# One jump into an arm for all eight experts, instead of one jump per expert

## The chip, the cores and the metric

One core of a Trainium2 chip runs the whole kernel. The metric is device microseconds from launch to end; lower is better.

## What is computed

```python
def reference(q, k, v, f, w_gate, w1, w2, capacity):      # cut to what matters
    # attention: 2 batches, 8 heads, 576 positions, 64 wide; f gives a decay; causal
    scores = q @ k.T / sqrt(64) + decay(f)
    x = softmax(scores) @ v            # -> 1152 tokens of 512
    # mixture of experts: 8 experts, top 1, capacity 288 tokens
    logits = x @ w_gate
    expert_idx = argmax(logits, axis=1);  gate = softmax(logits)[expert_idx]
    # a token takes the next free slot of its expert, and is dropped when there is none
    h = maximum(x_slots[e] @ w1[e], 0)     # w1: 512 x 1024
    y = h @ w2[e]                          # w2: 1024 x 512
    out[token] = gate[token] * y[expert_idx[token], slot[token]]
```

All is float32. How many tokens an expert gets is known only when the routing has been computed on the chip.

## The kernel before

The first 162 us of the span are attention, routing and the beginning of expert 0. That expert's tokens of the first batch, up to 128 of them, are worked through early (`early_*`), and only the rest counts as its load in what follows. The order of this stage comes from a planner in the kernel, and from 162 us on the program's own order holds for TensorE, ScalarE and VectorE.

**An arm.** The work of an expert is written for a fixed number of columns `n`. There are 14 arms: 128, 136, ... 208, 224, 256 and 288 columns. `route` counts the tokens of every expert (`ct`), compares each count with the arms' sizes (`cmp`, `acc`) and so gets the number of the smallest arm that holds them. The old kernel packs the eight numbers into two integers, four bits each (`arm`, two words). Every engine reads both words (`values_load`), and before each expert it cuts the expert's four bits out and jumps to that arm (`tc.Switch`). The code of all 14 arms stands one after the other, and behind the last one the engines meet again, with the next expert's switch. So TensorE, ScalarE, VectorE and GpSimd make two jumps per expert: from the switch to the arm, and from the arm's end to the place where all arms meet. SyncE does not jump: it only issues the weight loads, which stand outside the arms.

**Within an expert** (`expert`), TensorE does:
- L1 (`l1`): eight blocks `f` of 128 hidden rows, each 4 float32 matmuls over the tokens' 512 columns, which the profile counts as 8. Blocks go to three PSUM banks in turn (`a_ps`). ScalarE applies the ReLU and rounds to float32r (`hs[:, f, 0]`), VectorE writes the remainder (`hs[:, f, 1]`), and only then is the bank free.
- The second layer from float32r parts of `w2` and `hs`. At 128 columns it is `l2`, with tokens in the rows: 24 matmuls of 512 columns. At more columns it is `l2t`, with tokens in the columns: 4 blocks of 16 matmuls, then transposes of the result back to token rows (`y_t`).
- The transposes of the next expert's tokens (`x_prep`), which were gathered by index (`gather`, GpSimd).

`w2_split` makes the two parts of `w2`: ScalarE rounds (`w2s[:, 0, k]`), VectorE writes the remainder (`w2s[:, 1, k]`), GpSimd does one of eight. The splits for an expert stand among its own L1 blocks, two ahead of the first ReLU, and there is one buffer `w2s`. The scaled results of an expert go out by index (`y_out`, `scatter`) while the next one's L1 runs.

**Weights.** An expert has four tiles of 1 MB (`load_w`: `u` = 0, 1 are `w1`, 2, 3 are `w2`) in a ring for three experts. The tiles of expert `e + 2` are loaded at the start of expert `e`, into the place of expert `e - 1`.

Of the kernel before, what the change touches and what calls it, by code (L numbers as in the profile page):

```python
# [7 lines left out]
F32 = mybir.dt.float32  # L8
# [3 lines left out]
I32 = mybir.dt.int32  # L12
AF = mybir.ActivationFunctionType
ALU = mybir.AluOpType
AX = mybir.AxisListType
# [6 lines left out]
NE = 8  # L22
FF = 1024
NTOK = B * S
P = 128
# [10 lines left out]
NW1 = 3  # L36
XPD = (3, 3)
EQ = (1, 2)
# [33 lines left out]
ET = mybir.EngineType  # L72
# [9 lines left out]
def arm_sizes(cap):  # L82
    return [a for a in (*range(128, 216, 8), 224, 256) if a < cap] + [cap]
# [3 lines left out]
def attention_moe(ctx: ExitStack, tc: tile.TileContext, cap, kin, rawin, vin, f, c_iw, w1, w2,  # L87
                  c_mask, c_sel, c_idf, c_tri, c_one, c_pri, c_id, c_iota, c_slot, c_arms, out, dbg=None):
    nc = tc.nc
    ctx.enter_context(nc.allow_non_contiguous_dma("small strided loads"))  # L90
    ARMS = arm_sizes(cap)[:-1]
# [6 lines left out]
    wring = {}  # L98

    def open_ring(*keys):  # L100
        for r, u in keys:
            wring[r, u] = ctx.enter_context(tc.tile_pool(name=f"wraw{r}{u}", bufs=2))

    open_ring((0, 0), (0, 1), (1, 0))
    att = ExitStack()
# [299 lines left out]
    def route(b):  # L405
# [25 lines left out]
        for pb in range(b):  # L431
            for i in range(NT):
                r = ROWS[i]
# [72 lines left out]
        if b == 0:  # L506
            nc.vector.tensor_copy(tab[:, :, :, 1:], tg[:, :, :, 1:])
            if NCH > 1:
                nc.vector.tensor_copy(tab[:, :NCH - 1, :, 0], tg[:, 1:, :, 0])
            nc.vector.tensor_reduce(egat, tg[:, 0, :, 0], axis=AX.X, op=ALU.add)  # L510
            nc.vector.scalar_tensor_tensor(oh[:, :, 0], pos, float(P), oh[:, :, 0], op0=ALU.is_ge, op1=ALU.mult)
            emp = rt.tile([P, 1], F32, tag="eemp", name="eemp")
            nc.vector.tensor_scalar(emp, egat, 0.0, BIG, op0=ALU.is_le, op1=ALU.mult)
            nc.vector.tensor_tensor(esix, egix, emp, op=ALU.add)
        else:
            nc.vector.tensor_tensor(tab, tab, tg, op=ALU.add)
            cmp = rt.tile([1, NE, len(ARMS)], F32, tag="cmp", name="cmp")
            nc.vector.tensor_tensor(cmp, ct[:, :, None].to_broadcast([1, NE, len(ARMS)]),
                                    arms[:, None, :len(ARMS)].to_broadcast([1, NE, len(ARMS)]), op=ALU.is_gt)
            acc = rt.tile([1, NE], F32, tag="acc", name="acc")  # L520
            nc.vector.tensor_reduce(acc, cmp, axis=AX.X, op=ALU.add)
            nc.vector.tensor_tensor(acc, acc, arms[:, len(ARMS):], op=ALU.mult)
            pk = rt.tile([1, 2], F32, tag="pk", name="pk")
            nc.vector.tensor_reduce(pk, acc.rearrange("p (a e) -> p a e", a=2), axis=AX.X, op=ALU.add)
            nc.vector.tensor_copy(arm, pk)
        yield

    arms = const.tile([1, len(ARMS) + NE], F32, name="arms")
    arm = const.tile([1, 2], I32, name="arm")
    tab = const.tile([P, NCH, 3, NE], F32, name="tab")  # L530
    tab_i = const.tile([P, NCH, NE], F32, name="tab_i")
    prev = {}
# [56 lines left out]
        nc.vector.scalar_tensor_tensor(h[:, :, 1], a, 0.0, h[:, :, 0].bitcast(F32), op0=ALU.max, op1=ALU.subtract)  # L589

    def load_w(e, u, eng=nc.sync):
        t = wring[e % 3, u // 2].tile([P, 2048], F32, tag="w", name=f"wr{e}_{u}")
        if u < 2:
            eng.dma_start(t, w1[e, :, 2 * u:2 * u + 2, :].rearrange("p k f -> p (k f)"))
        else:
            eng.dma_start(t, w2[e, :, 4 * (u - 2):4 * (u - 2) + 4, :].rearrange("p k d -> p (k d)"))
        raws[e, u] = t
# [194 lines left out]
            t[z] += more  # L792
    act, dve = nc.scalar, nc.vector
    xc = range(min(2, NCH))
    ENG = [ET.PE, ET.Activation, ET.DVE, ET.Pool]

    def width(c):
        return min(P, SC - c * P)
# [25 lines left out]
    with tc.manual_schedule(engines=MAN):  # L824
        for e in (0, 1):
            for c in xc:
                gather(e, c, part(c))
        for k in range(FC):
            if k == EK:
                early_h(1)  # L830
            w2_split(0, k, nc.gpsimd if k in PK else dve)
        for k in range(FC):
            early_l2(k)
            for c in xc:
                if k == XE[c]:
                    x_prep(0, c, [act, dve], [spsum(f"x0{c}"), x_ps0 if c else spsum("x00b")])
            if k == XE[2]:
                packed = [nc.values_load(arm[0:1, z:z + 1], engines=tuple(ENG), min_val=0, max_val=16 ** 4 - 1)
                          for z in range(2)]
        act.activation(yss[0][0], ob_ps, AF.Copy, scale=egat)  # L840
    a_ps, y_ps, q_ps = banks[:3], banks[3:3 + NCH], banks[6:]

# [113 lines left out]
    with tc.manual_schedule(engines={ET.PE, ET.Activation, ET.DVE}):  # L956
        scatter(yss[0][0], esix[:, 0:1])
        for c in xc:
            dve.memset(y_ps[c], 0.0)
        for e in range(NE):  # L960
            for q in ((1, 2) if e == 0 else (e + 2,)):
                for u in range(NW1 if q == 1 else 0, 4 if q < NE else 0):
                    load_w(q, u, nc.sync if e else nc.gpsimd if u in EQ else nc.scalar)
            reg = ((packed[e // 4] >> 4 * (e % 4)) & 15).with_bounds(min_val=0, max_val=len(ARMS))
            for z in tc.Switch({g: reg for g in ENG}, len(ARMS) + 1):
                expert(e, (ARMS + [SC])[z])


def host_arrays(inputs):
# [25 lines left out]
    for i in range(NT):  # L995
# [16 lines left out]
        "c_one": np.ones((P, P), bf),  # L1012
        "c_pri": pri,
        "c_id": ids.astype(bf),
        "c_arms": np.array([arm_sizes(cap)[:-1] + [16 ** (e % 4) for e in range(NE)]], np.float32),
        "c_slot": np.arange(nch * P, dtype=np.float32).reshape(nch, P).T,
        "c_iota": np.broadcast_to(np.arange(cap).astype(np.float16), (P, cap)),
    }
# [20 lines left out]
```

## Time and profile before

| | |
|---|---|
| time, median of 3 runs | 381.79 us (381.0 to 383.2) |
| span of the profiled execution | 374.9 us (the page gives no other time of it) |
| TensorE busy | 311.3 us, 83% |
| VectorE / ScalarE / GpSimd busy | 182.3 / 153.5 / 118.5 us |
| L847, the matmuls of L1 | 81.4 us busy, 49.3 us idle before them |

The span runs from the first to the last instruction on the core. Busy time is summed over the whole span; what an engine waits for, and where, is in the views of the trace. In them `PE` is TensorE's matmuls, `PEld` its weight loads, DVE is VectorE, ACT ScalarE, POOL GpSimd and SP SyncE; a name with a small q behind it (`DVEq`) is the engine's sequencer. "Issue" is time in which an engine waited for nothing that the profile shows.

### The profile page before, as it was taken

What the parts mean: (1) busy time and instruction counts of PE and PEld (TensorE: products, weight loads), DVE (VectorE), ACT (ScalarE), POOL (GpSimd) and SP (SyncE); (2) the same over time, 40 slices, a digit from 0 to 9 for tenths busy, and PEclk for the clock granted to TensorE, in tenths of its full rate; (3) what the DMA queues carried; (4) which work ended last, traced back from release to release, by engine and by line L of the source; (5) the groups of instructions that cost most, each with busy time, mean ns of one, the idle gap of its engine ahead of it and who ended that gap; (6) DMA issues with size and microseconds to landing.
All of it is one profiled execution on the core that took longest, in us unless ns stands there. A gap on an engine that the chain in (4) does not pass through costs nothing.

```text
span 374.9 us, 6090 instructions
## 1 busy us (share of the span) xinstructions
PE 311.3 (83%) x1952; PEld 242.0 (65%) x1953; DVE 182.3 (49%) x605; ACT 153.5 (41%) x416; POOL 118.5 (32%) x142
## 2 busy tenths in 40 slices
PE   7999999999999999998659558758658397877980
PEld 3555666566565656988459558757557396877980
DVE  6565667579884654673116107208053251722520
ACT  4364666666663655352044116106241433513510
POOL 4458456673547100254022203203231220300301
PEclk8599999999996999999989969969969879996997
DMA  8993996799271941438992760583917600000001
GB/s 166 252 225 101 251 370 177 138 294 366 62 200 32 388 185 31 146 93 298 410 353 99 270 237 35 203 299 116 405 43 288 243 4 11 30 8 7 34 5 47
DMA packets 19747, 64.86 MB, mean 173 GB/s; under 512 B 3503, under 2 KB 7231, under 8 KB 15074
## 3 DMA queue, kind: packets, MB, share of 16 engines
q1 hardware_dynamic: 12354, 44.86, 36.5%
q0 software_dynamic: 6224, 15.21, 14.8%
q10 hardware_dynamic: 1040, 3.44, 2.5%
q8 instruction: 36, 0.59, 0.7%
q14 instruction: 93, 0.76, 0.6%
HBM read 56.38 MB, written 9.10 MB: 175 GB/s over the span
## 4 chain that ended last, share of the span: by engine, by line
PE 60%; issue 17%; DMA 14%; DVE 4%; ACT 1%; ACTq 1%; DVEq 1%; POOL 0%; SPq 0%; POOLq 0%
DMA out<-yss,six 12%; PE bank L847 11%; PE bank L312 9%; PE bank L269 8%; PE bank L339 7%; PE bank L268 6%; PE bank L882 4%; PE bank L355 3%; PE bank L862 3%; PE bank L577 2%; PE bank L781 1%; DMA wr<-in_w 1%; DMA raw<-in_rawin 1%; PE bank L399 1%; PE bank L819 1%
## 5 line engine op out<-in xcount | busy, mean ns | idle before, releaser
L847 PE MATMUL bank<-xs,wr 128*128 128x128 f32 (+3 forms) x512 | 81.4, 326 | 49.3 <-issue 20.5
L847 PEld LDWEIGHTS bank<-xs,wr 128*128 128x128 f32 x512 | 78.4, 222 | 53.3 <-issue 32.2
L777 DVE TENSOR_TENSOR w2s<-wr,w2s 128x512 fp32r<-128x512 f32 x56 | 44.7, 816 | 74.7 <-ACT w2s L776 54.5
L776 ACT ACTIVATE w2s<-wr 128x512 fp32r<-128x512 f32 x64 | 38.9, 628 | 71.7 <-PE bank L847 40.6
L294 ACT ACTIVATE p<-p,nb 128x128 f32<-128x128 f32 (+4 forms) x80 | 47.6, 597 | 9.6 <-DVE nb L282 9.5
L907 POOL DMA_INDIRECT out<-yss,six x16 | 16.0, 1002 | 108.8 <-ACT yss L899 101.3
L325 ACT ACTIVATE p<-bank 128x256 f32<-128x256 f32 (+4 forms) x56 | 24.8, 448 | 37.3 <-PE bank L312 36.8
L282 DVE CUSTOM_DVE_ANT_0 p<-bank,cd 128x128 f32<-128x128 f32 (+2 forms) x64 | 31.1, 486 | 18.4 <-PE bank L269 10.5
L312 PE MATMUL bank<-idf,p 128*128 128x128 f32 (+2 forms) x240 | 39.2, 276 | 0.4 <-ACT p L294 0.4
L268 PE MATMUL bank<-hi 128*128 128x128 f32 (+5 forms) x96 | 38.1, 397 | 1.6 <-POOL hi L245 1.6
L269 PE MATMUL bank<-kl,hi 64*128 64x128 f32 (+5 forms) x96 | 38.0, 396 | 0.0
L862 PE MATMUL bank<-hs,w2s 128*128 128x304 f32 (+2 forms) x128 | 34.5, 352 | 0.0
L852 ACT ACTIVATE hs<-bank 128x128 fp32r<-128x128 f32 (+3 forms) x64 | 18.5, 293 | 34.6 <-PE bank L847 30.6
L807 POOL DMA_INDIRECT xg<-x_dram,gix x16 | 15.6, 977 | 53.6 <-PE bank L819 19.2
L312 PEld LDWEIGHTS bank<-idf,p 128*128 128x128 f32 (+2 forms) x240 | 23.2, 139 | 14.3 <-issue 5.9
L864 PE MATMUL bank<-hs,w2s 128*128 128x152 f32 (+2 forms) x128 | 30.6, 239 | 0.0
L339 PE MATMUL bank<-p,v 128*64 128x320 f32 (+4 forms) x224 | 30.4, 390 | 0.0
L241 POOL TENSOR_TENSOR kl<-raw,hi 64x576 fp32r<-64x576 f32 x15 | 21.5, 1437 | 15.0 <-PE bank L269 6.4
L269 PEld LDWEIGHTS bank<-kl,hi 64*128 64x128 f32 (+1 forms) x96 | 16.2, 169 | 15.5 <-issue 11.6
L853 DVE SCALAR_TENSOR_TENSOR hs<-bank,hs 128x128 fp32r<-128x128 f32 (+3 forms) x64 | 19.0, 304 | 15.0 <-ACT hs L852 14.8
L882 PE MATMUL bank<-w2s,hs 128*128 128x512 f32 x96 | 25.2, 405 | 0.0
L268 PEld LDWEIGHTS bank<-hi 128*128 128x128 f32 (+1 forms) x96 | 17.4, 181 | 11.4 <-issue 3.9
(142 smaller groups left out, 414.4 us busy)
## 6 DMA issues: line engine op xcount, KB each, us to landing
wr<-in_w SPq DMA_DIRECT2D x27, 1024.0 KB, 12.7
raw<-in_rawin SPq DMA_DIRECT2D x7, 576.0 KB, 8.1
hi<-in_kin POOLq DMA_DIRECT2D x7, 576.0 KB, 12.4
cd<-c_dram SPq DMA_DIRECT2D x7, 576.0 KB, 9.5
wr<-in_w ACTq DMA_DIRECT2D x3, 1024.0 KB, 10.9
v<-in_vin SPq DMA_DIRECT2D x8, 320.0 KB, 4.3
out<-zero SPq DMA_DIRECT2D x8, 288.0 KB, 5.4
wr<-in_w POOLq DMA_DIRECT2D x2, 1024.0 KB
```

Of the source, the lines that this page charges most:

```text
L268: nc.tensor.matmul(s[:r, :cw], qa, hi[:, j, KA + c0:KA + c0 + cw], start=True, stop=False)
L269: nc.tensor.matmul(s[:r, :cw], qa[:D], kl[:, j, c0:c0 + cw], start=False, stop=True)
L282: nc.vector.tensor_tensor_reduce(p[:r, a:b], s[:r, a - c0:b - c0], src[:r, a:b], -0.125, 1e30 if a == 0 else nb[:r, 0:1], ALU.add, ALU.min ...
L294: nc.scalar.activation(p[:r, :w], p[:r, :w], AF.Exp, bias=bias, scale=-1.0, accum_out=rsum[:r, h // 2 % 2, i, h % 2:h % 2 + 1])
L312: nc.tensor.transpose(t[:kw, c * r:(c + 1) * r], p[:r, c * P:c * P + kw], idf[:r, :r])
L339: nc.tensor.matmul(o[a * D:a * D + D, c0:w], vt[g][:kw, a, c], ps[a][:kw, c, c0:w], start=(c == 0), stop=(c == nk - 1), skip_group_check=True)
L776: nc.scalar.activation(w2s[:, 0, k], raw, AF.Copy)
L777: eng.tensor_tensor(w2s[:, 1, k], raw, w2s[:, 0, k].bitcast(F32), op=ALU.subtract)
L847: nc.tensor.matmul(a[:, :n], w[:, (k % 2) * FF + f * P:(k % 2) * FF + (f + 1) * P], xs[e % 2][k // 2][:, k % 2, :n], start=(k == 0), stop= ...
L862: nc.tensor.matmul(av, w2s[:, 0, k, ds], hs[:, k, :, :n], start=(k == 0), stop=(k == FC - 1), skip_group_check=True)
L864: nc.tensor.matmul(av[:, 0], w2s[:, 1, k, ds], hs[:, k, 0, :n], start=False, stop=(k == FC - 1), skip_group_check=True)
L882: nc.tensor.matmul(y_ps[0][:n], hs[:, k, y, :n], w2s[:, z, k], start=(k == 0 and z + y == 0), stop=(k == FC - 1 and z == 1))
```

## The change

One number is kept instead of eight: the largest over the experts. There is one switch, ahead of expert 0, and each of the 14 arms holds all eight experts one behind the other, all with the same `n`. The weight loads now stand inside the arms, so SyncE jumps too (`ENG`). The weight tiles are twelve fixed buffers where the old kernel drew each from a pool; in both, two tiles share a ring place as before.

```diff
     def open_ring(*keys):
         for r, u in keys:
-            wring[r, u] = ctx.enter_context(tc.tile_pool(name=f"wraw{r}{u}", bufs=2))
+            pool = ctx.enter_context(tc.tile_pool(name=f"wraw{r}{u}", bufs=1))
+            wring[r, u] = [pool.tile([P, 2048], F32, name=f"wr{r}{2 * u + z}") for z in range(2)]
...
             acc = rt.tile([1, NE], F32, tag="acc", name="acc")
             nc.vector.tensor_reduce(acc, cmp, axis=AX.X, op=ALU.add)
-            nc.vector.tensor_tensor(acc, acc, arms[:, len(ARMS):], op=ALU.mult)
-            pk = rt.tile([1, 2], F32, tag="pk", name="pk")
-            nc.vector.tensor_reduce(pk, acc.rearrange("p (a e) -> p a e", a=2), axis=AX.X, op=ALU.add)
+            pk = rt.tile([1, 1], F32, tag="pk", name="pk")
+            nc.vector.tensor_reduce(pk, acc, axis=AX.X, op=ALU.max)
             nc.vector.tensor_copy(arm, pk)
...
     def load_w(e, u, eng=nc.sync):
-        t = wring[e % 3, u // 2].tile([P, 2048], F32, tag="w", name=f"wr{e}_{u}")
+        t = wring[e % 3, u // 2][u % 2]
...
-    ENG = [ET.PE, ET.Activation, ET.DVE, ET.Pool]
+    ENG = [ET.PE, ET.Activation, ET.DVE, ET.Pool, ET.SP]
...
-                packed = [nc.values_load(arm[0:1, z:z + 1], engines=tuple(ENG), min_val=0, max_val=16 ** 4 - 1)
-                          for z in range(2)]
+                chosen = nc.values_load(arm[0:1, 0:1], engines=tuple(ENG), min_val=0, max_val=len(ARMS))
...
-        for e in range(NE):
-            for q in ((1, 2) if e == 0 else (e + 2,)):
-                for u in range(NW1 if q == 1 else 0, 4 if q < NE else 0):
-                    load_w(q, u, nc.sync if e else nc.gpsimd if u in EQ else nc.scalar)
-            reg = ((packed[e // 4] >> 4 * (e % 4)) & 15).with_bounds(min_val=0, max_val=len(ARMS))
-            for z in tc.Switch({g: reg for g in ENG}, len(ARMS) + 1):
+        for q in (1, 2):
+            for u in range(NW1 if q == 1 else 0, 4):
+                load_w(q, u, nc.gpsimd if u in EQ else nc.scalar)
+        for z in tc.Switch({g: chosen for g in ENG}, len(ARMS) + 1):
+            for e in range(NE):
+                if e and e + 2 < NE:
+                    for u in range(4):
+                        load_w(e + 2, u)
                 expert(e, (ARMS + [SC])[z])
```

VectorE between expert 0 and expert 1, before: these rows are the last of expert 0's arms (the copies of the next x), the jump, the registers of the next switch, and the start of expert 1's first arm (L777 is the second half of `w2_split`, L853 the second half of `hs`).

```order
L804 COPY xs_1875<-bank_81 128x2x128
L804 COPY xs_1875<-bank_82 128x2x80
L1035 UNCONDITIONAL_BRANCH
L1035 SWITCH_STRIDE
L1035 REGISTER_ALU x2
L1035 ISA x2
L965 BRANCH_PREFETCH_HINT
L777 TENSOR_TENSOR w2s<-wr_2_1863,w2s 128x512 x2
L853 SCALAR_TENSOR_TENSOR hs<-bank_75,hs 128x128
```

The same place in the changed kernel, in the arm of 200 columns (there, lines behind L838 are one less):

```order
L867 TENSOR_REDUCE yt<-bank_86 128x200
L804 COPY xs_1879<-bank_81 128x2x128
L804 COPY xs_1879<-bank_83 128x2x80
L777 TENSOR_TENSOR w2s<-wr_1856,w2s 128x512 x2
L852 SCALAR_TENSOR_TENSOR hs<-bank_81,hs 128x200
```

The jump out, the switch's rows and the jump in are gone, and the first split of the next expert stands right behind the copies.

ScalarE at the one switch, before: the read of the arms' words, the scaling of expert 0's early rows, the three weight loads that ScalarE issues, the switch and the first arm.

```order
L838 TENSOR_LOAD arm x2
L840 ACTIVATE yss_1878<-bank_81,egat 128x512
L596 DMA wr_3_1979<-in_w 128x2048
L594 DMA wr_0_1981<-in_w 128x2048
L596 DMA wr_3_1987<-in_w 128x2048
L1035 SWITCH_STRIDE
L1035 REGISTER_ALU
L1035 ISA x2
L965 BRANCH_PREFETCH_HINT
L852 ACTIVATE hs<-bank_75 128x128
```

And in the changed kernel up to the switch, then the start of the tenth arm:

```order
L838 TENSOR_LOAD arm
L839 ACTIVATE yss_1882<-bank_87,egat 128x512
L596 DMA wr_1857<-in_w 128x2048
L594 DMA wr_1861<-in_w 128x2048
L596 DMA wr_1867<-in_w 128x2048
L1036 SWITCH_STRIDE
L1036 ISA x2
```

```order
L962 BRANCH_PREFETCH_HINT
L851 ACTIVATE hs<-bank_81 128x200
L851 ACTIVATE hs<-bank_82 128x200
```

The rows ahead of the switch are the same but for one read and one register row less; nine arms of eight experts each stand between them and the tenth arm.

SyncE's queue behind the attention stage, before: the last load that stands ahead of the experts, then the four loads of expert 3.

```order
L596 DMA wr_2_1863<-in_w 128x2048
L1035 UNCONDITIONAL_BRANCH
L594 DMA wr_0_3974<-in_w 128x2048
L594 DMA wr_1_3976<-in_w 128x2048
L596 DMA wr_2_3978<-in_w 128x2048
L596 DMA wr_3_3980<-in_w 128x2048
```

And now:

```order
L596 DMA wr_1856<-in_w 128x2048
L838 TENSOR_LOAD arm
L838 ISA x2
L1036 SWITCH_STRIDE
L1036 ISA x2
L962 BRANCH_PREFETCH_HINT
L594 DMA wr_66<-in_w 128x2048
L594 DMA wr_67<-in_w 128x2048
L596 DMA wr_71<-in_w 128x2048
L596 DMA wr_72<-in_w 128x2048
```

The four loads are the same; SyncE reads the arm's number and jumps before them.

## Rows read from the trace of the kernel before

**Rows 1.** The page: the span, and the chain of work that ended last, by engine.

```profile
span 374.9 us, 6090 instructions
...
PE 60%; issue 17%; DMA 14%; DVE 4%; ACT 1%; ACTq 1%; DVEq 1%; POOL 0%; SPq 0%; POOLq 0%
```

**Rows 2.** TensorE's matmuls in order of time over the expert stage: start us, us, line, operation, output<-input, weights, columns, how many; in brackets the idle time before and what ended it. L847 is L1, L882 the second layer at 128 columns, L862 (with L864) the second layer of the wider arms, L891 the transposes of its result.

```profile
168.65 2.84 PE L847 MATMUL bank<-xs,wr 128*128 128x128 f32 x24
172.81 4.73 PE L847 MATMUL bank<-xs,wr 128*128 128x128 f32 x40 [1.33 <-DVE hs L853]
177.30 2.33 PE L882 MATMUL bank<-w2s,hs 128*128 128x512 f32 x9
...
181.54 2.33 PE L882 MATMUL bank<-w2s,hs 128*128 128x512 f32 x9
188.47 4.96 PE L847 MATMUL bank<-xs,wr 128*128 128x152 f32 x24 [4.60 <-issue]
196.61 5.43 PE L847 MATMUL bank<-xs,wr 128*128 128x152 f32 x40 [3.18 <-DVE hs L853]
201.78 0.40 PE L862 MATMUL bank<-hs,w2s 128*128 128x304 f32 x1
...
209.94 0.38 PE L891 MATMUL bank<-idf,yt 128*128 128x128 f32 x2
...
218.88 5.11 PE L847 MATMUL bank<-xs,wr 128*128 128x152 f32 x24 [7.18 <-DMA wr<-in_w]
...
247.05 5.46 PE L847 MATMUL bank<-xs,wr 128*128 128x128 f32 x24 [5.60 <-issue]
...
268.55 2.92 PE L847 MATMUL bank<-xs,wr 128*128 128x128 f32 x24 [2.78 <-issue]
276.02 6.87 PE L847 MATMUL bank<-xs,wr 128*128 128x128 f32 x40 [4.56 <-DVE hs L853]
...
292.01 2.92 PE L847 MATMUL bank<-xs,wr 128*128 128x128 f32 x24 [2.81 <-issue]
...
315.14 3.50 PE L847 MATMUL bank<-xs,wr 128*128 128x160 f32 x24 [2.23 <-ACT w2s L776]
319.82 5.70 PE L847 MATMUL bank<-xs,wr 128*128 128x160 f32 x40 [1.18 <-DVE hs L853]
325.25 0.41 PE L862 MATMUL bank<-hs,w2s 128*128 128x320 f32 x1
...
333.53 0.38 PE L891 MATMUL bank<-idf,yt 128*128 128x128 f32 x2
...
334.47 0.82 PE L891 MATMUL bank<-idf,yt 128*128 128x128 f32 x6
339.97 13.72 PE L847 MATMUL bank<-xs,wr 128*128 128x200 f32 x64 [4.69 <-issue]
353.39 0.48 PE L862 MATMUL bank<-hs,w2s 128*128 128x400 f32 x1
...
362.91 1.20 PE L891 MATMUL bank<-idf,yt 128*128 128x128 f32 x8
```

**Rows 3.** The chain that ended last, in order of time: start us, us, what it spent it on. The first row is at the boundary from expert 0 to expert 1, the next three from expert 3 to expert 4, the last from expert 5 to expert 6.

```profile
188.08 6.69 issue
...
264.23 5.05 issue
269.29 0.04 DVEq L1035
...
269.64 4.63 issue
...
311.37 2.91 issue
```

**Rows 4.** Stretches of the trace: from and to in us, length, busy time of TensorE's matmuls and weight loads, DVE, ACT and POOL with counts, then the granted TensorE clock, the mean share of the 16 DMA engines, GB/s.

```profile
189.00:194.00 5.00, 4.43 (x24) 4.20 (x22) 0.00 (x0) 3.48 (x9) 0.35 (x1) 0.72 1.02 348
276.00:279.00 3.00, 2.98 (x14) 2.98 (x15) 2.45 (x6) 0.81 (x3) 0.00 (x0) 0.50 0.01 1
312.90:316.00 3.10, 0.86 (x7) 0.89 (x7) 0.00 (x0) 1.15 (x2) 0.00 (x0) 1.00 0.05 11
```

**Rows 5.** ScalarE in order of time in expert 7 (200 columns): the evictions of L1's blocks; two of the same kind stand between these two. Columns as in rows 2.

```profile
349.74 0.34 ACT L852 ACTIVATE hs<-bank 128x200 fp32r<-128x200 f32 x1
...
353.80 0.34 ACT L852 ACTIVATE hs<-bank 128x200 fp32r<-128x200 f32 x1 [1.02 <-PE bank L847]
```

**Rows 6.** All engines in order of time at the start of expert 7: ScalarE's first two splits and VectorE's first `hs`.

```profile
341.02 1.15 ACT L776 ACTIVATE w2s<-wr 128x512 fp32r<-128x512 f32 x2 [6.19 <-PE bank L847]
...
343.43 0.37 DVE L853 SCALAR_TENSOR_TENSOR hs<-bank,hs 128x200 fp32r<-128x200 f32 x1
```

**Rows 7.** All engines in order of time around the switch of expert 0: VectorE's last work ahead of it, ScalarE's last weight load ahead of it, ScalarE's first work behind it.

```profile
169.30 1.02 DVE L959 MEMSET bank<- 128x512 f32 x2 [0.87 <-DVE xs L804]
...
170.70 0.45 ACTq L596 DMA_DIRECT2D wr<-in_w  x1
...
172.09 0.61 ACT L852 ACTIVATE hs<-bank 128x128 fp32r<-128x128 f32 x3 [2.52 <-PE bank L847]
```

**Rows 8.** The page, DMA issues: what is loaded, by which queue, how many, KB each, median us from issue to landing.

```profile
wr<-in_w SPq DMA_DIRECT2D x27, 1024.0 KB, 12.7
```

**Rows 9.** Waits from 165 us to the end: who waited for whom, us in total, times, longest.

```profile
PE bank L847 <- DVE hs L853: 19.4, 7, 4.6
```

More of the change, by code (lines that the diff above doesn't have):

```diff
@@ L518, in route @@
             nc.vector.tensor_tensor(cmp, ct[:, :, None].to_broadcast([1, NE, len(ARMS)]),
-                                    arms[:, None, :len(ARMS)].to_broadcast([1, NE, len(ARMS)]), op=ALU.is_gt)
+                                    arms[:, None, :].to_broadcast([1, NE, len(ARMS)]), op=ALU.is_gt)
             acc = rt.tile([1, NE], F32, tag="acc", name="acc")
             nc.vector.tensor_reduce(acc, cmp, axis=AX.X, op=ALU.add)
-            nc.vector.tensor_tensor(acc, acc, arms[:, len(ARMS):], op=ALU.mult)
-            pk = rt.tile([1, 2], F32, tag="pk", name="pk")
-            nc.vector.tensor_reduce(pk, acc.rearrange("p (a e) -> p a e", a=2), axis=AX.X, op=ALU.add)
+            pk = rt.tile([1, 1], F32, tag="pk", name="pk")
+            nc.vector.tensor_reduce(pk, acc, axis=AX.X, op=ALU.max)
             nc.vector.tensor_copy(arm, pk)
         yield
-    arms = const.tile([1, len(ARMS) + NE], F32, name="arms")
-    arm = const.tile([1, 2], I32, name="arm")
+    arms = const.tile([1, len(ARMS)], F32, name="arms")
+    arm = const.tile([1, 1], I32, name="arm")
     tab = const.tile([P, NCH, 3, NE], F32, name="tab")
@@ L1014, in host_arrays @@
         "c_id": ids.astype(bf),
-        "c_arms": np.array([arm_sizes(cap)[:-1] + [16 ** (e % 4) for e in range(NE)]], np.float32),
+        "c_arms": np.array([arm_sizes(cap)[:-1]], np.float32),
         "c_slot": np.arange(nch * P, dtype=np.float32).reshape(nch, P).T,
```

## The prediction, made before the changed kernel was run

> **What bounds the kernel now.** I read the page first. In the chain that ended last, TensorE has 60% of the span and "issue" 17% [rows 1]: a sixth of the span is time in which an engine on the chain waited for nothing that the profile shows. To place it I read TensorE's order of time over the expert stage, which begins at 168.65 us with the first L1 matmul of expert 0 [rows 2]. Here the reader is to see two things.
>
> First, the widths. The experts' L1 matmuls are 128, 152, 152, 128, 128, 128, 160 and 200 columns wide: the old kernel fits every expert to its own tokens, and the largest arm is 200.
>
> Second, the holes. From expert 1 on each expert's L1 comes after 2.2 to 7.2 us of idle engine, and in most a second hole of 1.2 to 4.6 us stands between the first 24 matmuls and the other 40, put down to DVE's `hs` [rows 2]. Before the first kind nothing is late by the profile; in the second, DVE is late, because it had a hole of its own. The chain shows DVE's between experts 3 and 4: 5.05 us of issue, then 0.35 us in which its sequencer works on the next switch (269.29 to 269.64), then 4.63 us of issue [rows 3]. So each boundary has two jumps, out of the arm and into the next one. Their price goes with the DMA load: 6.69 us at the boundary where the DMA engines are full (share 1.02), 2.91 us where they are nearly empty (share 0.05) [rows 3, 4]. TensorE's holes are shorter than DVE's since it still has queued matmuls to run. So every engine is bound here by its jumps and not by its work, and that is what the change touches.
>
> **What the jumps cost now.** I take the work of an expert without holes and subtract. All stretches are at the full granted clock, from start to start [rows 2].
> - L1 is 64 matmuls; 40 of them take 177.30 - 172.81 = 4.49 us at 128 columns, 5.17 us at 152 and 5.43 us at 160. Times 1.6: 7.18, 8.27, 8.69 us. At 200 columns ScalarE's evictions, one per 8 matmuls, stand 353.80 - 349.74 = 4.06 us apart for three [rows 5]: 1.353 us x 8 = 10.83 us.
> - The second layer: 181.54 + 2.33 - 177.30 = 6.57 us at 128 columns (other form, preparation of the next x included); 8.16 us at 152; 8.28 us at 160; 362.91 - 353.39 = 9.52 us at 200.
> - The transposes after it, in the wide form alone: 334.47 + 0.82 - 333.53 = 1.76 us.
>
> An expert is then 13.75 us at 128, 18.19 at 152, 18.73 at 160 and 22.11 at 200. Experts 0 to 6 are 4 x 13.75 + 2 x 18.19 + 18.73 = 110.1 us of work, but they take 339.97 - 168.65 = 171.3 us. [...]
>
> **The change, part by part.**
>
> *Seven boundaries go: -61.2 us.* Inside the arm no engine jumps between experts. What must then be in time is ScalarE's and DVE's chain to the first `hs`, since TensorE has three banks and stops at the fourth block, 3 x 1.353 = 4.06 us after its L1 begins. Expert 7 shows this chain at the same width: from ScalarE's first split at 341.02 to DVE's `hs` at 343.43 + 0.37 = 343.80 it takes 2.78 us [rows 6]. Without jumps ScalarE is free as soon as it has copied the next x, before L1 begins, so the chain has 1.3 us to spare. I take no hole. The bound from the other side is the shortest hole left in the old trace, 1.18 us [rows 2]: 7 x 1.18 = +8.3 us.
>
> *Padding: +44.7 us.* Experts 0 to 6 run at 200 columns: 7 x 22.11 = 154.8 us for 110.1. ScalarE, DVE and POOL grow too, but expert 7 shows TensorE's L1 as the pace at that width: ScalarE's evictions wait for it.
>
> *Expert 7: -2.6 us.* It now enters without a hole. Its L1 took 353.39 - 339.97 = 13.42 us, all of it without a hole [rows 2]; at full clock it is 10.83 us, as above.
>
> *One entry: +8.3 us.* In the old kernel expert 0's arm is the first, right behind the switch, and ScalarE goes through in 172.09 - 171.15 = 0.94 us [rows 7]. Now all engines jump to the tenth arm. ScalarE can do so only after its three weight loads are issued, 170.70 + 0.45 = 171.15 [rows 7]. By then the loads are on the way, so I price the jump as the dear one: 171.15 + 0.4 + 6.69 = 178.2; plus one eviction of 0.34 (ScalarE) and 0.37 us (DVE) [rows 5, 6] TensorE's fourth block starts at 178.9. Without a hole it would start at 168.65 + 24 x 0.169 = 172.7: 6.2 us late. DVE, free at 170.32, is not later. Behind a hole of that size I charge a half clock as behind expert 4's, 6.87 - 4.73 = 2.1 us. TensorE's own jump, earlier and shorter, lies inside this. Bounds: with the cheapest jump (2.91 us) the block starts 2.4 us late and no clock is lost, +2.4 us; with DVE's two-jump hole of some 12 us the loss is 11.5 + 2.1 = 13.6 us.
>
> *Nothing for the loads and the registers.* SP now jumps too and issues the loads inside the arm. Expert 3's go when expert 0's L1 is over, near 187, and are used a period and a half later, near 243; a load lands in 12.7 us [rows 8]. If that cover went, expert 3 would wait up to those 12.7 us, once. One value is read where two were unpacked; the 0.35 us of switch rows per boundary lie in the 61.2.
>
> Sum: -61.2 + 44.7 - 2.6 + 8.3 = **-10.8 us**; the span goes from 374.9 to 364.1. The page gives no time of this execution but its span; the runs' median is 381.79 (381.0 to 383.2), 6.9 us above, and I leave that as it is, as the tail behind expert 7's last transposes: 381.79 - 10.8 = **371.0 us**.
>
> [...]
>
> **Rivals.**
> - *The holes are no jumps and stay.* Only the padding would be paid: 381.79 + 44.7 = 426 us. [...] Against it: the holes stand on each side of the register rows of the switch, and expert 0, whose arm needs no jump, has none on ScalarE. 0.01.
> - *The second hole stays (slower).* `w2s` has one buffer, so the splits begin only when the last second-layer matmuls are done. If the first `hs` still comes late as before, TensorE loses 19.4 us in seven holes [rows 9], and the sum is 371.0 + 19.4 = 390 us, more with a half clock. It decides from 10.8 / 7 = 1.5 us per boundary, which needs the chain to end 5.6 us after L1's start. For it: the trace names `hs` as what ended these holes. Against it: expert 7 has no such hole at the same width. 0.05. A shorter one of up to 1.2 us, to 379 us: 0.13.
> - *TensorE's code doesn't arrive in a straight line (slower).* One stall per expert at the cheapest jump's 2.91 us is 8 x 2.91 = 23 us: 394 us; it decides from 1.4 us. Against it: inside the arms of the wide experts there is no hole from the 25th matmul to the last transposes. 0.03.
> - *The entry hides:* 371.0 - 5.9 = 365 us. For it: the loads are only issued from 169 on. 0.12.
>
> That the arm is not 200 is no case: 200 is the widest of the eight shapes in the trace.
>
> **The numbers.** The forecast (367 to 374 us) has 0.66. The range runs from the hidden entry to the short holes, 365.5 to 379 us, and leaves out the slower rivals and the ends. A change of 0.5% (1.9 us) is about what can be told from none here: faster 0.87, same 0.05 (the upper end of the short holes), slower 0.08.
>
> **What would show it.** Eight experts with L1 at 200 columns, some 22.1 us from start to start from expert 1 on; no issue hole in TensorE but one at the entry; ScalarE's first eviction near 178 instead of 172.09; the clock at 1.00 from expert 1 on; loads of expert 3 from about 187. I am wrong if periods are 24 us or more, if DVE's `hs` still ends waits at the boundaries, or if issue holes stand inside the arm.

## The result and the profile after

The changed kernel takes 357.6 us (median of 5 runs, 357.3 to 363.9) beside 381.79 us for the old one (375.9 to 385.1): a ratio of 0.9455, with a 95% interval of 0.934 to 0.957. I forecast faster, but at 371.0 us, in a range of 365.5 to 379.0. The gain is 24.2 us by the medians and 357.6 / 0.9455 - 357.6 = 20.6 us by the ratio, where I had 10.8, so the size is wrong and the time lies below the range.

In some executions, of either kernel, the clock granted over the whole run is lower and the time longer (0.949 and 363.94 us beside 0.960 to 0.970 and 357.3 to 358.9 us in the changed kernel, 0.855 and 396.78 us beside 0.920 and 376.18 us in the old one); the ratios leave those out and the medians do not, the first profile of the changed kernel (a span of 362.1 us) is such a one, and so I take lengths of the stage before the experts from its other profiles.

The page of the changed kernel: the span, two DMA queues that carry instructions (packets, MB, share of 16 engines), and the two groups that answer to what the old kernel waited for.

```profile
span 362.1 us, 6223 instructions
...
PE 344.1 (95%) x2144; PEld 279.8 (77%) x2145; DVE 191.9 (53%) x612; ACT 164.2 (45%) x436; POOL 118.6 (33%) x142
...
q8 instruction: 19, 0.31, 0.3%
q14 instruction: 25, 0.20, 0.2%
...
L846 PE MATMUL bank<-xs,wr 128*128 128x200 f32 x512 | 90.0, 337 | 4.5 <-issue 2.9
...
L777 DVE TENSOR_TENSOR w2s<-wr,w2s 128x512 fp32r<-128x512 f32 x56 | 46.4, 845 | 9.6 <-ACT w2s L776 9.5
```

The same rows before:

```profile
q8 instruction: 36, 0.59, 0.7%
q14 instruction: 93, 0.76, 0.6%
...
L777 DVE TENSOR_TENSOR w2s<-wr,w2s 128x512 fp32r<-128x512 f32 x56 | 44.7, 816 | 74.7 <-ACT w2s L776 54.5
```

Of what the instruction queues moved less than half is left, 0.51 MB for 1.35. L1's matmuls had 49.3 us of idle time before them and have 4.5. VectorE waited 54.5 us for ScalarE's half of the splits and waits 9.5.

TensorE's order of time answers to [rows 2]; L846 is L1, L861 the first row of the second layer, L890 the transposes. First from the entry to expert 2, then expert 7.

```profile
171.21 0.95 PE L781 MATMUL bank<-w2s,he 128*128 128x512 f32 x3
175.03 5.98 PE L846 MATMUL bank<-xs,wr 128*128 128x200 f32 x24 [2.87 <-issue]
182.66 7.03 PE L846 MATMUL bank<-xs,wr 128*128 128x200 f32 x40 [1.65 <-DVE hs L852]
...
200.49 10.99 PE L846 MATMUL bank<-xs,wr 128*128 128x200 f32 x64
211.18 0.49 PE L861 MATMUL bank<-hs,w2s 128*128 128x400 f32 x1
...
220.70 0.38 PE L890 MATMUL bank<-idf,yt 128*128 128x128 f32 x2
...
222.29 10.99 PE L846 MATMUL bank<-xs,wr 128*128 128x200 f32 x64
...
331.22 10.99 PE L846 MATMUL bank<-xs,wr 128*128 128x200 f32 x64
...
351.42 1.20 PE L890 MATMUL bank<-idf,yt 128*128 128x128 f32 x8
```

The reader is to see that both kinds of holes are gone from expert 1 on: L1 is one run of 64 matmuls, and from start to start it is (331.22 - 200.49) / 6 = 21.79 us. Both remain once, at the entry. The windows say the same (from and to, length, busy TensorE matmuls and weight loads, DVE, ACT, POOL, granted clock, DMA share, GB/s):

```profile
222.30:331.20 108.90, 108.90 (x722) 108.90 (x721) 53.33 (x105) 47.59 (x116) 23.66 (x23) 1.00 0.38 145
```

Over five experts TensorE is busy all of the time, at the full clock, with the DMA engines at 0.38. One caution: the chain that ended last still shows 19% of issue, but its longest pieces lie inside such a stretch, as at 296.81:

```profile
296.81 16.55 issue
```

By the window above TensorE works all through it, so nothing stands still there.

### The profile page after: what moved, and what is told of

Same layout as the page of the kernel before. It is cut to its first block, busy times and chain, and to the rows that moved or that the text cites. A ratio compares the mean times of both kernels' runs of the same rounds, so it can differ in the third digit from the quotient of the medians.

```text
span 362.1 us, 6223 instructions
## 1 busy us (share of the span) xinstructions
PE 344.1 (95%) x2144; PEld 279.8 (77%) x2145; DVE 191.9 (53%) x612; ACT 164.2 (45%) x436; POOL 118.6 (33%) x142
## 4 chain that ended last, share of the span: by engine, by line
PE 70%; issue 19%; POOL 3%; DVE 3%; DMA 2%; ACTq 1%; ACT 0%; SPq 0%; POOLq 0%; DVEq 0%
PE bank L846 14%; PE bank L313 9%; PE bank L861 9%; PE bank L270 8%; PE bank L340 8%; PE bank L269 7%; PE bank L863 4%; PE bank L356 3%; PE bank L400 2%; DMA raw<-in_rawin 2%; POOL out L906 1%; DVE w2s L777 1%; PE bank L577 1%; PE bank L819 1%; POOL w2s L777 1%
## 5 line engine op out<-in xcount | busy, mean ns | idle before, releaser
L846 PE MATMUL bank<-xs,wr 128*128 128x200 f32 x512 | 90.0, 337 | 4.5 <-issue 2.9
L846 PEld LDWEIGHTS bank<-xs,wr 128*128 128x128 f32 x512 | 88.0, 193 | 5.2 <-issue 3.3
L861 PE MATMUL bank<-hs,w2s 128*128 128x400 f32 x256 | 76.6, 367 | 0.0
L863 PE MATMUL bank<-hs,w2s 128*128 128x200 f32 x256 | 65.2, 255 | 0.0
L777 DVE TENSOR_TENSOR w2s<-wr,w2s 128x512 fp32r<-128x512 f32 x56 | 46.4, 845 | 9.6 <-ACT w2s L776 9.5
L863 PEld LDWEIGHTS bank<-hs,w2s 128*128 128x128 f32 x256 | 49.0, 191 | 0.0
L861 PEld LDWEIGHTS bank<-hs,w2s 128*128 128x128 f32 x256 | 48.1, 188 | 0.0
L851 ACT ACTIVATE hs<-bank 128x200 fp32r<-128x200 f32 x64 | 21.4, 337 | 41.8 <-PE bank L846 26.8
L852 DVE SCALAR_TENSOR_TENSOR hs<-bank,hs 128x200 fp32r<-128x200 f32 x64 | 23.0, 362 | 29.8 <-ACT hs L851 29.6
L870 DVE TENSOR_TENSOR yt<-bank,yt 128x200 f32<-128x200 f32 x24 | 8.8, 366 | 46.9 <-ACT yt L869 46.9
L869 ACT ACTIVATE yt<-bank 128x200 f32<-128x200 f32 x24 | 8.1, 337 | 47.6 <-PE bank L863 47.6
```

The costliest lines, as they stand in the source:

```text
L777: eng.tensor_tensor(w2s[:, 1, k], raw, w2s[:, 0, k].bitcast(F32), op=ALU.subtract)
L846: nc.tensor.matmul(a[:, :n], w[:, (k % 2) * FF + f * P:(k % 2) * FF + (f + 1) * P], xs[e % 2][k // 2][:, k % 2, :n], start=(k == 0), stop= ...
L861: nc.tensor.matmul(av, w2s[:, 0, k, ds], hs[:, k, :, :n], start=(k == 0), stop=(k == FC - 1), skip_group_check=True)
L863: nc.tensor.matmul(av[:, 0], w2s[:, 1, k, ds], hs[:, k, 0, :n], start=False, stop=(k == FC - 1), skip_group_check=True)
```

## The experiments

All times are medians of runs beside the old kernel on the same chip. L781 is the last work of the stage before; from its end to the end of the span is the expert stage, the quantity that the change touches. It is 374.9 - 168.8 = 206.1 us in the old kernel and 362.1 - 172.16 = 189.9 us in the changed one.

**The changed kernel again, without an edit (`again`).**

> The changed kernel as it is, once more, for a second profile. In the first one the span is 362.1 us, while other runs of it are 6 us shorter. Theory A (the attention stage of that one execution was slow, clock 0.74 from 20 to 40 us, and the expert stage is what it is): the expert stage, from the last early matmul to the end, is again 190 us (189.9), periods of 21.8 us from expert 1 on, and a shorter span comes from an earlier start of it, near 166 to 169 us. Theory B (the expert stage itself varies): the stage is some 184 us and begins near 172 us.

Measured: 358.21 us (356.7 to 358.8), a ratio of 0.9487 (0.9388 to 0.9586). The expert stage is 354.9 - 166.13 = 188.8 us, 1.1 us from the first profile's, although the span is 7.2 us shorter. So the expert stage repeats, and what differs lies ahead of it.

**All experts on the largest arm, with the jumps left in (`pad`).** The old kernel; `route` packs the largest of the eight numbers eight times.

```diff
-            nc.vector.tensor_tensor(acc, acc, arms[:, len(ARMS):], op=ALU.mult)
+            top = rt.tile([1, 1], F32, tag="top", name="top")
+            nc.vector.tensor_reduce(top, acc, axis=AX.X, op=ALU.max)
+            nc.vector.tensor_tensor(acc, top.to_broadcast([1, NE]), arms[:, len(ARMS):], op=ALU.mult)
```

> The kernel before, with its eight switches, but every expert takes the arm of the largest count (200 columns): the padding alone. Theory J (the holes are the jumps' own, and as long as before): the padding costs 7 x 21.8 - 110.1 = 42.5 us and expert 0 pays one jump more: 420 to 430 us. Rival H (in the narrow arms TensorE only waited for VectorE and ScalarE, so that part of the wider work fits into the holes): 395 to 410 us, with shorter holes than 8.7 us per boundary.

Measured: 432.86 us (429.1 to 439.5), a ratio of 1.1439 (1.103 to 1.1848). TensorE's order of time, L1 of experts 0, 1, 2, 6 and 7 (here L849):

```profile
169.96 5.74 PE L849 MATMUL bank<-xs,wr 128*128 128x200 f32 x24 [3.12 <-issue]
...
202.02 6.76 PE L849 MATMUL bank<-xs,wr 128*128 128x200 f32 x24 [7.81 <-issue]
...
235.43 7.12 PE L849 MATMUL bank<-xs,wr 128*128 128x200 f32 x24 [7.62 <-DMA wr<-in_w]
...
365.48 13.72 PE L849 MATMUL bank<-xs,wr 128*128 128x200 f32 x64 [5.15 <-issue]
...
395.37 12.44 PE L849 MATMUL bank<-xs,wr 128*128 128x200 f32 x64 [5.21 <-issue]
```

With the same 200 columns as in the changed kernel a period is (395.37 - 169.96) / 7 = 32.2 us (29.8 to 33.5) instead of 21.79. The padding is paid, and 10.4 us of boundary on top of it, so the holes belong to the jumps and not to the widths. They are longer than the old kernel's (171.3 - 110.1) / 7 = 8.7 us, and the time lies above theory J's 420 to 430 us, which had them as long as before. The fixed weight buffers, which came with the change, have no run of their own; `noload`, below, draws no weight tile from expert 3 on, and VectorE's two jumps still take 5.5 and 7.0 us there at two boundaries, so the buffers are at most a part of it.

**The straight line without the padding (`fit`).** The changed kernel; the tenth arm gives each expert its own width, written out for the token counts of these inputs.

```diff
+FIT = [128, 152, 152, 128, 128, 128, 160, 200]
...
-                expert(e, (ARMS + [SC])[z])
+                expert(e, FIT[e] if z == 9 else (ARMS + [SC])[z])
```

> The changed kernel, but the tenth arm holds the eight experts at their own widths (128, 152, 152, 128, 128, 128, 160, 200, fixed for this input): the jumps alone, no padding. Theory J, with the work without holes as worked out from the trace (13.75, 18.19, 18.73 us): 42.5 us less than the changed kernel, near 315 us. Rival H (at 128 columns VectorE's split and eviction, some 1.1 us per block, are slower than TensorE's 0.9, and the first eviction comes late): L1 of the 128-column experts near 9 to 11 us instead of 7.2, 320 to 330 us. Rival D (4 MB of weights per 14 us don't arrive in time): TensorE waits for loads, over 325 us.

Measured: 319.66 us (314.0 to 337.2), a ratio of 0.8461 (0.8208 to 0.8715). L1 of experts 1, 2, 3, 6 and 7:

```profile
186.33 8.43 PE L847 MATMUL bank<-xs,wr 128*128 128x152 f32 x64
204.26 8.43 PE L847 MATMUL bank<-xs,wr 128*128 128x152 f32 x64
222.19 7.67 PE L847 MATMUL bank<-xs,wr 128*128 128x128 f32 x64
...
262.94 8.85 PE L847 MATMUL bank<-xs,wr 128*128 128x160 f32 x64
281.40 10.99 PE L847 MATMUL bank<-xs,wr 128*128 128x200 f32 x64
```

There are no holes at these widths either, nor at experts 4 and 5 between, and the time is near theory J's 315 us. L781's counterpart ends at 164.47, so the expert stage is 312.2 - 164.47 = 147.7 us. That is 188.8 - 147.7 = 41.1 us below `again`: the padding by itself, where I had 44.7. From expert 1's L1 to the end it is (354.9 - 193.35) - (312.2 - 186.33) = 35.7 us, where the sum had 36.3; the rest of the miss lies at expert 0, where TensorE's second hole is 2.37 us in `fit` and 0.44 in `again`, so part of the wider work falls into the entry's wait. Against the old kernel the stage is 206.1 - 147.7 = 58.4 us shorter: the jumps by themselves with the entry paid, where the sum had 61.2 + 2.6 - 8.3 = 55.5. `pad` keeps the jumps and `fit` leaves the padding out; the two parts of the sum are each seen alone.

**The arm right behind the switch (`first`, and `first_b` with more runs).** The changed kernel with the arms below 200 columns left out, so that the arm taken is the first.

```diff
-    return [a for a in (*range(128, 216, 8), 224, 256) if a < cap] + [cap]
+    return [a for a in (200, 208, 224, 256) if a < cap] + [cap]
```

> The changed kernel with only the arms from 200 columns up (200, 208, 224, 256, 288): nothing that runs is changed, but the arm that is taken now stands right behind the switch. Theory J (the hole at the entry is the fetch of far code): ScalarE's first eviction comes about 1 us after its last weight load is issued, TensorE has no issue hole at expert 0, and 5 to 6.5 us go: 351 to 353 us. Rival W (expert 0 waits for its weights or for the three loads that ScalarE issues): the hole stays, 357 us.

> The changed kernel without the nine arms below 200 columns, so that the arm taken stands right behind the switch, as in the run named first (351.6 us of span, median 355.74 of four). Theory E (the far jump at the entry costs about 4.5 us, and nothing else differs): from the end of L781 to the end of the span 184 to 185.5 us, no issue hole of TensorE at the entry, ScalarE's first eviction within 1 us of the end of its last load issue; median 353 to 355 us, so 3.5 to 5 us below after_c, its interval clear of after_c's. Rival (the 4.5 us lie within what the attention stage varies by): medians within 2 us of each other.

> The changed kernel again, beside the two kernels below on the same chip. Theory A (the expert stage is the same in every execution, the attention stage ahead of it varies): median 357 to 359.5 us; from the end of the last split ahead of the experts (L781) to the end of the span 188 to 190 us; periods of 21.8 us from expert 1 on; TensorE's issue hole at the entry 2.8 to 3.1 us. Rival (the entry's price varies with the DMA load as the boundaries' did in the kernel before): that stretch differs by 2 us or more from the 188.8 and 189.9 us seen so far.

Measured: `first` 355.74 us (351.9 to 358.5; theory J had 351 to 353); `first_b` 354.58 us, a ratio of 0.935 (0.9252 to 0.9448), beside `after_c`, the changed kernel, with 359.9 us, a ratio of 0.9491 (0.940 to 0.9582). By the medians and by the ratios that is some 5.3 us; the intervals overlap a little, so theory E's clear interval was not met. No kernel here that takes any token counts has a lower ratio (`fit` is written for these counts, and `noload`, below, computes with other weights). ScalarE (activations, and ACTq its load issues) in `after_c`, the same eviction in `again`, and then `first_b`:

```profile
164.62 0.69 ACT L839 ACTIVATE yss<-bank,egat 128x512 f32<-128x512 f32 x1 [0.58 <-PE bank L781]
...
166.46 1.24 ACTq L596 DMA_DIRECT2D wr<-in_w  x1
175.11 0.80 ACT L851 ACTIVATE hs<-bank 128x200 fp32r<-128x200 f32 x3 [9.79 <-PE bank L846]
```

```profile
174.67 0.80 ACT L851 ACTIVATE hs<-bank 128x200 fp32r<-128x200 f32 x3 [7.81 <-DMA wr<-in_w]
```

```profile
169.15 0.69 ACT L839 ACTIVATE yss<-bank,egat 128x512 f32<-128x512 f32 x1 [0.58 <-PE bank L781]
...
170.51 0.44 ACTq L596 DMA_DIRECT2D wr<-in_w  x1
171.81 0.56 ACT L851 ACTIVATE hs<-bank 128x200 fp32r<-128x200 f32 x2 [1.97 <-issue]
```

From the end of the last issue to the first eviction it is 175.11 - 167.70 = 7.41 us with nine arms in between and 171.81 - 170.95 = 0.86 us without (0.85 in `first`). The trace names a TensorE bank as what ended ScalarE's wait in `after_c`, and a weight load in `again` and in the first profile. But behind the same three issues the same eviction waits for neither when the arm is near, so `first`'s rival W fell. The expert stage is 355.2 - 164.59 = 190.6 us in `after_c` and 352.1 - 169.11 = 183.0 us in `first_b` (351.6 - 167.3 = 184.3 us in `first`), where L1 of expert 0 follows L781 without a hole:

```profile
168.16 0.95 PE L781 MATMUL bank<-w2s,he 128*128 128x512 f32 x3
168.95 10.99 PE L846 MATMUL bank<-xs,wr 128*128 128x200 f32 x64
```

Theory A's 188 to 190 us were missed by 0.6, upwards; its median too, by 0.4. Theory E's 184 to 185.5 us were missed by 1.0, downwards; its median was met.

**The old kernel again (`before_b`).**

> The kernel before, once more, for a second profile of it. Its runs so far lie from 376 to 399 us, those of the changed kernel from 357 to 359 but for one, and the one profile of before that the prediction was worked out from is of an execution near the low end (span 374.9). Theory P (the price of the jumps varies from execution to execution): a longer execution has the same stage up to expert 0 within 4 us and a longer expert stage (206 us in the first profile), with holes of 9 to 11 us per boundary instead of 8.7. Rival C (the clock is lower all along): the first 165 us are longer in proportion, and the holes are as they were.

Measured: 380.61 us (377.9 to 392.2), a ratio of 0.9995 (0.9929 to 1.0061) against the same kernel. Its profile has a span of 382.6 us, and the time of that execution is 384.41: 1.8 us lie around the span, as in every other execution here that has both (1.7 to 2.0). The expert stage is 382.6 - 170.1 = 212.5 us, 6.4 more than in the first profile. The chain's two pieces at the boundary after expert 0 were 5.29 and 6.69 us there, and after expert 1 5.89 and 6.81; here they are:

```profile
183.53 5.59 issue
189.57 6.99 issue
214.46 7.05 issue
221.86 6.41 issue
```

From the start of expert 0's L1 to the start of expert 7's it is 348.06 - 170.16 = 177.9 us instead of 171.3, so with 110.1 us of work the seven boundaries cost 67.8 us instead of 61.2: 9.7 us each, as theory P had it, while the stage before was only 1.3 us longer. So the boundaries' price is not one number, even for one kernel.

**The jumps without the loads (`noload`).** The old kernel, in which experts 3 to 7 take the tiles of the expert three before them, and no weights are loaded for them: experts 3 to 7 so use weights that aren't theirs.

```diff
-                    load_w(q, u, nc.sync if e else nc.gpsimd if u in EQ else nc.scalar)
+                    if e:
+                        raws[q, u] = raws[q - 3, u]
+                    else:
+                        load_w(q, u, nc.gpsimd if u in EQ else nc.scalar)
```

> The kernel before, without the weight loads from expert 3 on: experts 3 to 7 work with the weights that lie there (the output is another one). Its eight switches stay. Theory L (a jump is dear because the code is fetched through the same DMA engines as the weights): at the boundaries from expert 2 on the issue pieces are near 3 us, as where the DMA engines were empty (2.91 us), not 4.6 to 6.8; 15 to 25 us less than before, and runs closer together. Rival N (the jump costs what it costs): the issue pieces stay at 4 to 7 us, and the time within 5 us of before.

Measured: 353.06 us (350.6 to 356.8), a ratio of 0.9315 (0.9054 to 0.9576). The windows of three boundaries, expert 0 to 1, 3 to 4 and 5 to 6, in the old kernel and then in `noload` (columns as above; each window runs from the start of VectorE's jump out to the end of its jump in, or some tenths beyond):

```profile
182.30:194.80 12.50, 6.53 (x31) 5.71 (x29) 0.04 (x1) 4.06 (x9) 2.89 (x3) 0.86 1.02 376
264.20:274.30 10.10, 4.48 (x31) 3.70 (x29) 0.03 (x1) 3.78 (x9) 2.93 (x3) 0.97 0.81 320
...
311.30:318.00 6.70, 4.46 (x28) 3.86 (x28) 0.07 (x1) 2.32 (x6) 0.00 (x0) 1.00 0.03 7
```

```profile
181.80:191.80 10.00, 5.37 (x23) 4.77 (x23) 0.07 (x1) 1.85 (x4) 1.86 (x2) 0.83 0.56 188
...
253.20:258.70 5.50, 4.46 (x31) 3.70 (x29) 0.02 (x1) 3.79 (x9) 2.25 (x3) 1.00 0.31 85
...
287.70:294.70 7.00, 4.55 (x29) 3.95 (x29) 0.07 (x1) 2.42 (x6) 0.00 (x0) 1.00 0.03 8
```

Where loads of a later expert ran in the old kernel, VectorE's two jumps fall once these are gone: from 12.5 to 10.0 us as the share falls from 1.02 to 0.56, and from 10.1 to 5.5 us as it falls from 0.81 to 0.31. At the boundary where neither kernel loads anything (0.03) they cost the same, 6.7 and 7.0 us. So of the boundary from expert 3 to 4 about half goes with the loads and half is there without them. The price doesn't go to nothing: theory L's pieces near 3 us came (from expert 3 to 4 in the chain of `noload`, below), and the gain was a little more than its 15 to 25 us. That 5.5 us at 0.31 lie below 7.0 at 0.03 says little, as the second boundary leads into another arm, of 160 columns.

```profile
253.22 2.26 issue
...
255.84 2.80 issue
```

**Two tries at the entry that gave nothing (`inarm`, `hinted`).** `inarm`: the five loads that ScalarE and GpSimd issue ahead of the switch are issued by SyncE in the arm.

```diff
-        for q in (1, 2):
-            for u in range(NW1 if q == 1 else 0, 4):
-                load_w(q, u, nc.gpsimd if u in EQ else nc.scalar)
...
+                if e == 0:
+                    for q in (1, 2):
+                        for u in range(NW1 if q == 1 else 0, 4):
+                            load_w(q, u)
```

> The changed kernel, but the eight loads ahead of the switch (of experts 1 and 2; ScalarE issues three, GpSimd two) are issued by SyncE in the arm. So ScalarE reaches the switch some 2 us earlier, and its jump falls before these loads run. Theory L: the entry (5.4 us above the period of 21.8 in the second profile of the changed kernel) gets 3 to 4 us shorter: 354 us. Rival N: only the 2 us of the issuing go, ScalarE's hole stays at 6 us or more: 356 to 358 us.

Measured: 361.3 us (357.5 to 365.0), a ratio of 0.9531 (0.9347 to 0.9714). Neither theory's time came. ScalarE is free 0.7 us behind L781's end instead of 2.2 to 3.1, but its first eviction comes 9.5 us behind L781's end, where the other profiles have 8.5 to 10.5, and TensorE's own hole is 6.43 us for 2.9 to 3.1:

```profile
177.98 12.80 PE L846 MATMUL bank<-xs,wr 128*128 128x200 f32 x64 [6.43 <-issue]
```

`hinted`: all engines get a hint for the arm's code as soon as they have read its number.

```diff
+                tc.switch_hint({g: chosen for g in ENG}, len(ARMS) + 1, "arm")
```

> The changed kernel with a prefetch hint for the tenth arm on every engine, right behind the read of the arm's number, some 3 us ahead of ScalarE's jump. If a hint fetches the code ahead: ScalarE's first eviction comes 3 us earlier, 354 us. If it does not (in the kernel before each arm's first row is a hint for its exit, and the exit still cost VectorE 5.05 us): 357 to 358 us, no change.

Measured: 366.98 us (two runs near 359, two near 376); the profile's span is 357.2 us. ScalarE's first eviction comes at 176.99, 6.65 us after its last issue, and TensorE's hole is 3.10 us with an expert stage of 189.2 us: no gain.

**Both at the entry (`both`).** The arms of `first` and the loads of `inarm`.

> As first_b, and the eight loads of experts 1 and 2 that stand ahead of the switch (three on ScalarE's queue, two on GpSimd's) are issued by SyncE inside the arm. Theory S (the three issues hold ScalarE for some 2 us between its last work of the attention stage and its first eviction, and the loads come in time from within the arm): ScalarE's first eviction 1 to 2 us earlier than in first_b against the end of L781, and the median 0.5 to 2 us lower, 352 to 354 us. Theory T (what TensorE waits for at the entry is its own first matmuls, L781 and the weights of expert 0, so ScalarE has time): within 0.5% of first_b. Theory W (loads that start later arrive late for expert 1 or 2): an idle time of TensorE of 2 us or more ended by DMA wr or by the splits of w2s in expert 1 or 2, and 1 to 4 us slower than first_b.

Measured: 362.68 us (three runs from 352.95 to 354.8, three from 370.6 to 373.5), a ratio of 0.9354 (0.9234 to 0.9474), as `first_b`'s. ScalarE:

```profile
168.09 0.69 ACT L839 ACTIVATE yss<-bank,egat 128x512 f32<-128x512 f32 x1 [0.58 <-PE bank L781]
169.50 0.34 ACT L851 ACTIVATE hs<-bank 128x200 fp32r<-128x200 f32 x1 [0.73 <-PE bank L846]
```

Its first eviction is 1.45 us behind L781's end instead of 2.70, and the expert stage is 351.1 - 168.05 = 183.05 us as in `first_b`. Theory T holds: with the arm near, TensorE waits for nobody at the entry, as L1 of expert 0 is one run of 64 matmuls from 167.89 us, and L781 ends at 168.05. No loads came late: from 165 us on the trace names no wait of TensorE.

## Why the prediction was wrong in size

**Right.** *Seven boundaries are jumps.* `pad` and `fit` separate them from the padding, and not one hole is left behind the entry; DVE's chain to the first `hs` was in time, as worked out: L1 is one run of 64 matmuls from expert 1 on. *Padding:* 41.1 us for 44.7, and 35.7 for 36.3 from expert 1 on. *Loads in the arm cost nothing:* from 165 us on, `again` names one wait for a weight load, 7.8 us of ScalarE's, and it is the one at the entry. *ScalarE's jump:* I had 178.2 - 171.15 = 7.05 us from its last issue to the first eviction; the runs have 6.35 (`again`), 6.79 and 7.41 us. With the arm right behind the switch it is 0.86 us (`first_b`), so the price goes with the arm's place; the instruction queues moved 0.51 MB for 1.35.

**Wrong: the sum's foot.** The step "6.9 us above, and I leave that as it is". It read the gap between the profiled span (374.9) and the median (381.79) as work around the span. That is 1.7 to 2.0 us in all runs, so the profiled execution took some 376.7 us, and the median was that of an execution 5.1 us longer. A difference taken from one execution was put on the time of another. `before_b`, a longer execution too, shows where such a surplus can lie: its boundaries, which the change takes away, cost 6.6 us more. With the right foot the forecast is 376.7 - 10.8 = 365.9 us, still too high; the rest is in the terms.

**Wrong: three terms of the expert stage, and one that wasn't there.** Between the first profile of the old kernel and `again`, the span falls 374.9 - 354.9 = 20.0 us and not 10.8. The 9.2 us between lie in four places; with the foot's 5.1 that is 14.3, and as `again`'s execution (356.68 us) is 0.9 us below the median, it comes to the 13.4 us by which I missed:
- *Entry, 3.0 us.* From L781's end to expert 1's L1 I had 199.06 - 168.80 = 30.3 us; `again` has 193.35 - 166.13 = 27.2 (28.3 in the first profile, 29.2 in `after_c`). The fourth block's start was met: 10.1 us behind L781's end, measured 9.4 to 11.4. What failed is the 2.1 us of half clock behind it. The clock is low, 0.74, but over the 24 matmuls ahead, behind which TensorE waits for ScalarE anyway; the 40 behind run at 1.00. In `again`, L781's end and expert 1's L1, then the windows of those two stretches:

```profile
165.20 0.93 PE L781 MATMUL bank<-w2s,he 128*128 128x512 f32 x3
...
193.35 10.99 PE L846 MATMUL bank<-xs,wr 128*128 128x200 f32 x64
```

```profile
169.00:175.50 6.50, 5.98 (x24) 5.70 (x24) 0.39 (x2) 0.80 (x3) 1.89 (x3) 0.74 0.99 386
175.60:182.00 6.40, 6.40 (x38) 6.40 (x39) 1.89 (x6) 1.35 (x4) 0.29 (x1) 1.00 1.01 415
```

- *Periods, 1.9 us.* 21.79 us for 22.11, six times. L1 takes 211.18 - 200.49 = 10.69 us where ScalarE's evictions gave 10.83, and the transposes 222.29 - 220.70 = 1.59 where expert 6 gave 1.76; the second layer takes 220.70 - 211.18 = 9.52, as expert 7 gave it.
- *Expert 7, 1.5 us.* From its L1 to the end it takes 30.81 us for 32.3; of the first profile's 1.45, 1.3 us is the tail behind the last transposes (10.7 us for 12.0), which I had left as it was.
- *The stage before, 2.7 us.* L781 ends at 166.13 for 168.80. I had no term for it, and it is no effect shown: in the changed kernel's three profiles this end lies at 164.6, 166.1 and 172.2.

**The rivals.** "The holes stay" and "code doesn't arrive in a straight line" fell with the windows at full busy time; "second hole stays" fell, and the short hole too: it stands once, at the entry. "The entry hides" didn't come about: by `first` and `first_b` the far jump costs 188.8 to 190.6 less 183.0 to 184.3, so 4.5 to 7.6 us of the expert stage.

**A reading too wide.** "Before the first kind nothing is late by the profile" does not hold for two of the seven holes: for expert 2 the rows name a weight load (7.18 us), for expert 6 a split (2.23 us) [rows 2]. In `noload` the hole before expert 2's L1 is 4.65 us, all of it issue, so most of that one is the jump's as well.

**Open.** Why the old kernel's runs spread from 376 to 402 us isn't settled: `before_b` shows dearer boundaries, but at 384.41 us, and no profile fell into one of the longest. That the price is the fetching of code is my reading of the near arm (0.86 us for 6.35 to 7.41), the loads (10.1 us with them, 5.5 without, from expert 3 to 4) and the instruction queues (0.51 MB for 1.35); it is not shown, as no row has a jump that waits for a packet.

## What to carry to other kernels

Count a run-time switch per iteration as two jumps on each engine that takes part, and price them from the trace where the DMA engines are busy and where they are idle: one jump for the whole loop paid here for 41 us of padding. Put the arm that is taken most often right behind the switch; this is shown where an engine comes to the switch in a straight line (0.86 us for 6.35 to 7.41). Behind a jump it is not: from expert 3 to 4 the old kernel jumps into its first arm too, and VectorE's piece behind the register rows was 4.63 us [rows 3], and 2.80 us in `noload`. Before a sum made on one profile is set against a median, ask for that execution's own time.

## What the runs showed of the hardware

- A jump's price has a part that goes with the DMA load and a part that stays: VectorE's two jumps took 5.5 to 7.0 us at DMA shares of 0.31 and below, 10.0 to 10.4 us at five boundaries from 0.56 to 0.82, and 12.5 and 13.1 us at 1.02 (old kernel, `before_b` and `noload`). The share alone does not set it: from expert 1 to 2 the old kernel's took 13.1 us at 0.82.
- The arm's place: from ScalarE's last load issue to its first eviction 0.86 us with the arm right behind the switch, 6.35 to 7.41 us with nine arms in between.
- The hint for the arm's code, given ahead of the loads, gave nothing: 6.65 us from the last issue to the first eviction, and 6.35 to 7.41 without it.
- With ScalarE's loads out of its way TensorE's own hole at the far jump was longer, 6.43 us for 2.9 to 3.1 (one profile of `inarm`; why is open).
